# Attention and expert layer on one core: last transposes on TensorE, and the order of the first pairs and of the last pair's side work

## The chip, the cores and the metric

The kernel runs on one core of a Trainium2 chip. The core's engines run side by side, each through its own list of instructions in order: TensorE (PE, matmuls into the PSUM banks), VectorE (DVE), ScalarE (ACT), GpSimd (POOL), and SyncE (SP), which here only starts transfers. Transfers can be started from SP's, ScalarE's or GpSimd's queue and share 16 DMA engines. Engines wait for one another on semaphores. The metric is the device time of one execution, in microseconds (us), the median over several runs.

## What is computed

Attention over 8 batches, 8 heads and 1152 keys, with queries averaged in pairs (576 queries a head), and then a layer of 8 experts of which each of the 4608 tokens takes one.

```python
q_pool = q.reshape(B, H, S // 2, 2, D).mean(axis=3)          # B=8, H=8, S=1152, D=64
scores = np.matmul(q_pool, k.transpose(0, 1, 3, 2)) / np.sqrt(D)
attn = softmax(scores)                                       # over the 1152 keys
x = concat_heads(np.matmul(attn, v))                         # 4608 tokens x 512
logits = x @ w_gate + modality_bias[modality_id]
e_idx, gate = argmax(logits), softmax(logits)[argmax]
out[mask_e] = gate * (relu(x[mask_e] @ w1[e]) @ w2[e])       # for each expert e, F=1024
```

All data are float32. The kernel keeps the precision with 16-bit operands: each operand is split into a high half and a remainder (hi and lo, vh and vl, xh and xl), and a product is two or three matmuls.

## The kernel before

**Attention.** The work goes in 32 pairs: two batches of one head, their 64 rows side by side on the 128 partitions. A pair takes 18 steps (NSTEP), nine for each of its two heads, so the loop has 576 steps, and a written order (ORD, three strings used in turn) says what a step emits: "s" one bank of scores (`scores`: L821 and L822 into psc, exponential on ScalarE at L823), "v" one fifth of a value product (`pv`: L868 to L870), "M" and "X" pieces of the next pair's pass for the row maxima (`maxpass`: L759 and L760), "J" one step of a job, "F" what falls due. TensorE, ScalarE, VectorE and GpSimd keep exactly this order; SP's order is left to a scheduler. What belongs to other pairs is put at fixed steps by constants: T_KQ and T_K2 (loads of K and Q), T_SPLIT, T_QH, T_HI, T_LO (splits), T_MAX and T_M1 (row maxima), T_PLACE, T_P1 and T_P2 (`place`, copies by SP into the score operands B1 and B2), V0 and T_SQ to T_VS (the scale of the values and their split in VH, vl and VS).

**The exponentials** come out as 32-bit integers whose low half is turned into a third operand Pl by ScalarE ('A', L804) or VectorE ('D', L806), as LOWS lists it, and LOWS_LAST for the last pair.

**The first pair** is made in line ahead of the loop: K in thirds and Q in halves are loaded by turns; `first_max` takes the maxima of five of nine query tiles with 15 matmuls (L779) and reductions (L780); `row` reduces them (L731), transposes the result on TensorE (L735), scales it (L744) and has SP copy it as a row into B2. The first scores need this row. T_PRE pieces of the maxima of the other four tiles are emitted before the loop.

**After each two pairs** `split_xl` splits their outputs in xh and xl, and two DMA transposes (L851) make xt, from which `logits` takes the gate's logits (18 matmuls, L238). For the last pair the two transposes are issued from ScalarE's queue. When all four parts of a group of 1152 tokens are there, `route` computes expert and gate; after three groups `first_list` makes the list of tokens of the first six blocks of experts (`operands` on VectorE at L463 to L471, matmuls at L490, indices at L502 to L509). These run as generators, one piece at a time: a `yield n` puts the next piece n steps later. At step T_G0 of the last pair `gather_first` drains what is left of them and gathers the first block's tokens. T_X0 starts the turning of this block (`turn`), T_W0 its weights' loads, T_W1 their splits, W1D the steps by which the remainder follows.

**Experts.** 18 blocks of 256 tokens and one of 128: `gemm1` (L1191 to L1193), relu on ScalarE and its remainder on VectorE (hh L1196, hl L1197), `gemm2` (L1237 to L1239). The weights come in pieces of 512 KB through a ring of five buffers, each split by ScalarE and VectorE (L1174, L1175). Tokens are gathered by GpSimd, split (xs, L1141) and turned by DMA transposes on SP (L1147). Each half piece of a product calls `beside`, which takes one step of what is left from the attention: after SW empty steps the last `logits`, the last group's `route` and `other_list`.

Of the kernel before, what the change touches and what calls it, by code (L numbers as in the profile page):

```python
# [22 lines left out]
P = 128  # L23
# [19 lines left out]
T_LIST = -126  # L43
RS = 4
# [8 lines left out]
LOWS_LAST = (((0, 576, 'D', 1), (576, 1152, 'D', 2), (1152, 1728, 'A', 3)),)  # L53
D0 = 5
T_RT = 25
D2 = 3
T_K2 = 3
T_F = 7
T_P2 = 10
T_P1 = 5  # L60
T_M1 = 3
# [8 lines left out]
V0 = (0, 1, (2, 3), 4, (4, 5))  # L70
# [14 lines left out]
T_G0 = 0  # L85
T_X0 = 9
# [24 lines left out]
SW = 8  # L111
PR = 2
NF = 4
T_W0 = (1, 1, 2, 3)
W1D = 1
T_W1 = (7,9,11,13)
# [19 lines left out]
LLA = 4  # L136
# [3 lines left out]
T_PRE = 9  # L140
# [11 lines left out]
class Router:  # L152
# [11 lines left out]
    def setup(self, ids, w_gate, bias):  # L164
# [16 lines left out]
        nc.gpsimd.affine_select(out=self.up, in_=self.up, pattern=[[1, P]], compare_op=ALU.is_gt, fill=0.0, base=0, channel_multiplier=-1)  # L181
        self.on = con.tile([P, P], BF16, name="on")
# [46 lines left out]
    def logits(self, g, cc, x, w):  # L229

        nc = self.nc
        if g not in self.lg:
            self.lg[g] = self.keep.tile([P, NT, 3 * E], F32, name="lg")
# [297 lines left out]
def attention(tc, ctx, att, ident, npairs, xpool, on_two, on_split, on_scale, jobs, side, set_pm, started, ahead, hip):  # L531
# [54 lines left out]
    def split_q(p):  # L586
# [6 lines left out]
        if p == 0:  # L593
            q = t.rearrange("p (w n) -> p w n", w=2)
            for i in range(2):
                nc.vector.tensor_tensor(q[:, 0, half_q(i)], q[:, 0, half_q(i)], q[:, 1, half_q(i)], op=ALU.add)
        else:
            nc.gpsimd.tensor_tensor(t[:, 0:SQ], t[:, 0:SQ], t[:, SQ:S], op=ALU.add)
# [106 lines left out]
    def values(p, i, lo):  # L705
# [8 lines left out]
        if lo:  # L714
# [6 lines left out]
    def shifted(p):  # L721

        need(p, "vh0", "vh1")
        made.add((p, "vs"))
        nc.vector.tensor_single_scalar(flat(VS[p % 3])[:, :, 0:D], flat(VH[p % 3])[:, :, 0:D], 2.0 ** -16, op=ALU.mult)

    def row(p, mp, u0, u1):
# [13 lines left out]
        def put(pt):  # L741
# [3 lines left out]
            move(B2[p % 2][D:D + 1, 2 * S + u0 * P:2 * S + u1 * P], mr[0:n])  # L745
# [27 lines left out]
    def first_max(p):  # L773

        s = st[p]
        mp = sm.tile([P, 9, 3], F32, name="mp")
        for i, (u, t) in enumerate([(u, t) for us in ((0, 1), (2, 3, 4)) for t in range(3) for u in us]):
            pt = ps_sc.tile([P, 512], F32, name="psc") if i % 2 else ps_max.tile([P, 512], F32, name="pm")
            nc.tensor.matmul(pt[:, 0:384], QB[p % 2][:, u], s["hi"][:, t * 384:(t + 1) * 384], start=True, stop=True)  # L779
            nc.vector.tensor_reduce(mp[:, u, t:t + 1], pt[:, 0:384], op=ALU.max, axis=AX.X)  # L780
        row(p, mp, 0, 5)()
        return mp

    def scores(p, j, r):
# [10 lines left out]
        lows = (LOWS_LAST if p == npairs - 1 else LOWS)  # L795
# [47 lines left out]
    def split_xl(p, x2):  # L843
# [4 lines left out]
        if p % 2:  # L848
            xt = [xpool.tile([P, NT, P], F16, name=f"xt{i}", bufs=1) for i in range(2)]
            for i, x in enumerate((xh, xl)):  # L850
                (nc.scalar if p == npairs - 1 else nc.sync).dma_start_transpose(out=xt[i], in_=x.rearrange("p t d -> p (t d)"))  # L851
            on_split(p // 2, xt, st[p - 1]["both"].bitcast(F32))
# [133 lines left out]
    for p in range(npairs):  # L986
        b = NSTEP * p
        go = lambda t, f, *a, p=p, b=b, **k: at(b + t, p, lambda: f(p, *a), **k)
        if p > 1:
            d = D2 if p == 2 else 0  # L990
            go(T_K2 - b if p == 2 else T_KQ, load_kq, end=False)
            go(T_SPLIT + d, split_q)
            go(T_QH + d, split_qh)
            for i in range(2):
                go(T_HI[i] + d, split_hi, i)
            for i in range(3 if LOC else 7):
                go(T_LO[LOCI[i] if LOC else i] + d, split_lo, i)
            go(T_MAX + d, lambda p: mxq.append(maxpass(p)), end=False)
# [6 lines left out]
        sq, power_, vh, vs, vl = (T_SQ, T_POW, T_VH, T_VS, T_VL) if p else V0  # L1005
# [337 lines left out]
def attention_moe(tc, att, ids, w_gate, bias, w1, w2, out):  # L1343
    nc = tc.nc
    with ExitStack() as ctx:
# [106 lines left out]
```

## Time and profile before

| | |
|---|---|
| median of 3 runs (lowest, highest) | 1191.72 us (1188.98 to 1196.6) |
| the profiled execution | 1192.5 us |
| its span, first to last instruction | 1190.7 us |
| mean granted TensorE clock | 0.984 |
| first scores, first exponential | 19.42, 20.38 us |
| first matmul of the experts | 771.99 us |
| HBM read, written | 146.11 MB, 19.18 MB |

In the profile a row of the timeline is: start, duration, engine, line, operation, output<-input, shape, count, and in brackets the idle time before it with what ended that. "PEld" is the loading of weights into TensorE, "ACTq" and "SPq" are issues on a queue. In the view of stretches the columns are the stretch, its length, busy time with number of instructions of PE, PEld, DVE, ACT and POOL, the granted TensorE clock, the share of the DMA engines' time and GB/s.

### The profile page before, as it was taken

The numbers are of one execution on the slowest core, as the hardware profiler recorded it, in microseconds if no ns is written. First come the engines' busy times: TensorE is split into PE (matmuls) and PEld (weight loads), VectorE is DVE, ScalarE is ACT, GpSimd is POOL, SyncE is SP. The second block draws the span as 40 slices with busy tenths as digits, with TensorE's granted clock in tenths as the row PEclk, the third lists the DMA queues.
The fourth block names the chain that finished last, engine by engine and source line by source line (L and its number), as shares of the span: only waits on it lengthen the run. The fifth ranks groups of instructions, "written<-read, shape, count | busy, mean of one in ns | idle before, by whom it ended". The sixth has DMA issues, their size and how long they took to land. (4 is left out here: it accounts for less than half of the span.)

```text
span 1190.7 us, 36600 instructions
## 1 busy us (share of the span) xinstructions
PE 1117.9 (94%) x14944; PEld 817.8 (69%) x14944; DVE 984.2 (83%) x2033; ACT 918.1 (77%) x1461; POOL 408.3 (34%) x384
## 2 busy tenths in 40 slices
PE   5898999999999999999999989888999999999994
PEld 2566777777777777777777767755767666676763
DVE  6988899899999899999999999649996756667571
ACT  5778999999999999999998888736556656566561
POOL 6253444444434444434445331123213121211200
PEclk7999999999999999999999999899999999999998
DMA  7657768758759669668668534499999999999970
GB/s 221 183 134 169 156 170 203 149 159 199 165 156 217 150 164 205 148 163 187 169 167 186 145 93 110 142 186 279 230 300 309 298 278 278 286 280 274 261 243 22
DMA packets 177937, 233.25 MB, mean 196 GB/s; under 512 B 94719, under 2 KB 129167, under 8 KB 177760
## 3 DMA queue, kind: packets, MB, share of 16 engines
q1 hardware_dynamic: 169264, 210.46, 68.7%
q0 software_dynamic: 6128, 19.78, 6.5%
q10 hardware_dynamic: 2368, 0.59, 0.8%
q8 instruction: 119, 1.95, 0.7%
q14 instruction: 58, 0.48, 0.1%
HBM read 146.11 MB, written 19.18 MB: 139 GB/s over the span
## 5 line engine op out<-in xcount | busy, mean ns | idle before, releaser
L823 ACT ACTIVATE Pe<-psc 128x432 int32<-128x432 f32 x768 | 380.8, 526 | 71.4 <-PE psc L822 59.4
L760 DVE TENSOR_REDUCE mp<-pm 128x1 f32<-128x512 f32 x566 | 370.6, 684 | 9.7 <-PE pm L759 4.1
L868 PE MATMUL xp<-VH,Pe 128*128 128x65 f16 x2880 | 374.2, 194 | 0.5 <-ACT xfirst L1099 0.5
L870 PE MATMUL xp<-VS,Pl 128*128 128x65 f16 x2880 | 373.7, 193 | 0.0
L869 PE MATMUL xp<-vl,Pe 128*128 128x64 f16 x2880 | 372.4, 192 | 0.5 <-issue 0.5
L869 PEld LDWEIGHTS <-Pe 128*128 128x128 f16 x2880 | 268.3, 98 | 89.4 <-issue 1.6
L868 PEld LDWEIGHTS <-Pe 128*128 128x128 f16 x2880 | 272.8, 98 | 56.2 <-issue 18.6
L822 PE MATMUL psc<-B 65*128 65x432 f16 (+2 forms) x1152 | 307.4, 289 | 1.4 <-DMA B<-mr 1.1
L821 PE MATMUL psc<-B 128*128 128x432 f16 (+2 forms) x1152 | 306.9, 288 | 1.5 <-ACT Pe L823 1.5
L870 PEld LDWEIGHTS <-Pl 128*128 128x128 f16 x2880 | 267.2, 97 | 0.0
L759 PE MATMUL pm<-hi,QB 128*128 128x512 f16 x566 | 215.4, 382 | 19.3 <-DVE mp L760 16.3
L804 ACT ACTIVATE Pl<-Pe 128x1152 f16<-128x1152 uint16 (+1 forms) x192 | 220.6, 1149 | 6.1
L717 POOL TENSOR_SCALAR VH<-rawv,sc 128x512 f16<-128x512 f32 (+1 forms) x60 | 103.4, 1734 | 180.3 <-PE xp L870 110.6
L633 POOL TENSOR_TENSOR lo<-rawk,hi 128x576 f16<-128x576 f32 (+1 forms) x68 | 89.0, 1312 | 221.0 <-ACT hi L617 170.7
L1191 PE MATMUL ph<-xpart,w1h 128*128 128x256 f16 x544 | 148.9, 274 | 6.7 <-DVE hl L1197 5.6
L1192 PE MATMUL ph<-xpart,w1h 128*128 128x256 f16 x544 | 148.9, 274 | 0.0
L1193 PE MATMUL ph<-xpart,w1l 128*128 128x256 f16 x544 | 148.9, 274 | 0.0
L822 PEld LDWEIGHTS <-B 65*128 65x128 f16 x1152 | 113.7, 99 | 25.6 <-issue 2.4
L821 PEld LDWEIGHTS <-B 128*128 128x128 f16 x1152 | 113.2, 98 | 11.6 <-issue 6.2
L806 DVE TENSOR_SCALAR Pl<-Pe 128x576 f16<-128x576 uint16 x198 | 104.4, 528 | 15.5 <-ACT Pe L823 14.3
L1237 PE MATMUL po<-w2h,hh 128*128 128x512 f16 x296 | 112.9, 381 | 0.0
L1238 PE MATMUL po<-w2l,hh 128*128 128x512 f16 x296 | 112.7, 381 | 0.0
(254 smaller groups left out, 1782.3 us busy)
## 6 DMA issues: line engine op xcount, KB each, us to landing
w2r<-in_w_dram SPq DMA_DIRECT2D x76, 512.0 KB
w1r<-in_w_dram SPq DMA_DIRECT2D x72, 512.0 KB
rawv<-in_att_dram SPq DMA_DIRECT2D x32, 576.0 KB
B<-hi SPq DMA_DIRECT2D x128, 144.0 KB
rawq<-in_att_dram SPq DMA_DIRECT2D x31, 576.0 KB
rawk<-in_att_dram SPq DMA_DIRECT2D x31, 576.0 KB
B<-qh SPq DMA_DIRECT2D x128, 72.0 KB
B<-lo SPq DMA_DIRECT2D x64, 144.0 KB
```

What stands on the lines that cost most here:

```text
L759: nc.tensor.matmul(pm, QB[p % 2][:, u], s["hi"][:, t * 512:(t + 1) * 512], start=True, stop=True)
L760: nc.vector.tensor_reduce(mp[:, u, t:t + 1], pm, op=ALU.max, axis=AX.X)
L804: nc.scalar.activation(low, rest, AF.Copy, scale=LOW)
L821: nc.tensor.matmul(o, b1[:, ks], b1[:, qs], start=True, stop=False, skip_group_check=True)
L822: nc.tensor.matmul(o, b2[:, ks], b2[:, qs], start=False, stop=True, skip_group_check=True)
L823: nc.scalar.activation(Pe[:, D + x0:D + x1], pt, AF.Exp, scale=1.0 / 16)
L868: nc.tensor.matmul(out, Ph[:, qs], vh[:, c, j, 0:D + 1], start=c == 0 and g == 0, stop=False, skip_group_check=True)
L869: nc.tensor.matmul(out[:, 0:D], Ph[:, qs], vl[:, c, j], start=False, stop=False, skip_group_check=True)
L870: nc.tensor.matmul(out, Pl[:, qs], vs[:, c, j, 0:D + 1], start=False, stop=c == NKC - 1, skip_group_check=True)
L1191: nc.tensor.matmul(o, hi[:, c, fs], xh[:, :, c], start=c == 0, stop=False)
L1192: nc.tensor.matmul(o, hi[:, c, fs], xl[:, :, c], start=False, stop=False)
L1193: nc.tensor.matmul(o, lo[:, c, fs], xh[:, :, c], start=False, stop=c == 3)
```

## The change

The last pair's xh and xl are transposed by matmuls with an identity (`turned`) in place of the two DMA transposes, as part of the last job, which starts after 3 empty steps in place of 8. The first pair's loads, query sums and maxima are emitted in a new order; its row goes by ScalarE's queue; seven pieces of its other maxima move into the loop. The second pair's square, scale and split move from the first steps to steps 7 to 15. For the first two pairs the values' remainder is two operations on GpSimd in place of one on VectorE, and the first pair's VS is made on ScalarE. `route` and the lists wait fewer steps between pieces. In the last pair ScalarE's part of Pl goes to VectorE, and the first block's gather, turning and splits get other steps. LOWS0, for the first pair, equals what was used before.

```diff
-T_LIST = -126
-RS = 4
+T_LIST = -127
+RS = 2
...
-LOWS_LAST = (((0, 576, 'D', 1), (576, 1152, 'D', 2), (1152, 1728, 'A', 3)),)
+LOWS_LAST = (((0, 864, 'D', 1), (864, 1728, 'D', 3)),)
...
-D2 = 3
-T_K2 = 3
+D2 = (4, 2, 2, 3, 6)
+T_K2 = 0
...
-T_P2 = 10
-T_P1 = 5
-T_M1 = 3
+T_P2 = 4
+T_P1 = 7
+T_M1 = 5
...
-V0 = (0, 1, (2, 3), 4, (4, 5))
+V0 = (0, 1, (2, 3), 3, (3, 4))
+V1 = (7, 9, (12, 13), 14, (14, 15))
+LOWS0 = (((0, 1152, 'A', 2), (1152, 1728, 'D', 3)),)
...
-T_G0 = 0
-T_X0 = 9
+T_G0 = -1
+T_X0 = 7
...
-SW = 8
+SW = 3
...
-T_W0 = (1, 1, 2, 3)
-W1D = 1
-T_W1 = (7,9,11,13)
+T_W0 = (1, 3, 2, 3)
+W1D = 0
+T_W1 = (6, 4, 10, 11)
...
-LLA = 4
+LLA = 1
...
-T_PRE = 9
+T_PRE = 2
...
+        self.id16 = con.tile([P, P], F16, name="id16")
+        nc.gpsimd.tensor_copy(self.id16, self.ident)
...
-    def logits(self, g, cc, x, w):
+    def turned(self, x, o):
 
         nc = self.nc
+        for i in range(2):
+            for a, b in ((0, 4), (4, 8), (8, NT)):
+                pt = self.pm(0)[:, 0:(b - a) * P].rearrange("p (t n) -> p t n", n=P)
+                for t in range(a, b):
+                    nc.tensor.matmul(pt[:, t - a], x[i][:, t], self.id16, start=True, stop=True, skip_group_check=True)
+                (nc.vector.tensor_copy if i else nc.scalar.copy)(o[i][:, a:b], pt)
+                yield
+
+    def logits(self, g, cc, x, w, to=None):
+
+        nc = self.nc
+        if to:
+            yield from self.turned(x, to)
+            x = to
...
-            for i in range(3):
-                if i < 2:
+            for x, i in ((q, 0), (k, 0), (k, 1), (q, 1), (k, 2)):
+                if x is q:
                     nc.sync.dma_start(out=two(q)[:, :, half_q(i)], in_=two(att[p, :, S:2 * S])[:, :, half_q(i)])
-                nc.sync.dma_start(out=k[:, i * 384:(i + 1) * 384], in_=att[p, :, i * 384:(i + 1) * 384])
+                else:
+                    nc.sync.dma_start(out=k[:, i * 384:(i + 1) * 384], in_=att[p, :, i * 384:(i + 1) * 384])
...
-        if lo:
+        if lo and p < 2:
+            nc.gpsimd.tensor_scalar(v, v, s["sc"], None, op0=ALU.mult)
+            nc.gpsimd.tensor_tensor(flat(s["vl"][:, c]), v, vh, op=ALU.subtract)
+        elif lo:
             nc.vector.scalar_tensor_tensor(flat(s["vl"][:, c]), v, s["sc"], vh, op0=ALU.mult, op1=ALU.subtract)
...
-        nc.vector.tensor_single_scalar(flat(VS[p % 3])[:, :, 0:D], flat(VH[p % 3])[:, :, 0:D], 2.0 ** -16, op=ALU.mult)
+        o, v = (flat(x[p % 3])[:, :, 0:D] for x in (VS, VH))
+        if p:
+            nc.vector.tensor_single_scalar(o, v, 2.0 ** -16, op=ALU.mult)
+        else:
+            nc.scalar.activation(o, v, AF.Copy, scale=2.0 ** -16)
...
-            move(B2[p % 2][D:D + 1, 2 * S + u0 * P:2 * S + u1 * P], mr[0:n])
+            (nc.sync if p or u0 else nc.scalar).dma_start(out=B2[p % 2][D:D + 1, 2 * S + u0 * P:2 * S + u1 * P], in_=mr[0:n])
...
             nc.vector.tensor_reduce(mp[:, u, t:t + 1], pt[:, 0:384], op=ALU.max, axis=AX.X)
+            yield
         row(p, mp, 0, 5)()
-        return mp
...
+            both = st[p - 1]["both"].bitcast(F32)
+            if p == npairs - 1:
+                on_split(p // 2, (xh, xl), both, xt)
+                return
             for i, x in enumerate((xh, xl)):
-                (nc.scalar if p == npairs - 1 else nc.sync).dma_start_transpose(out=xt[i], in_=x.rearrange("p t d -> p (t d)"))
-            on_split(p // 2, xt, st[p - 1]["both"].bitcast(F32))
+                nc.sync.dma_start_transpose(out=xt[i], in_=x.rearrange("p t d -> p (t d)"))
+            on_split(p // 2, xt, both)
...
-    for i in range(3):
+    first = first_max(0)
+    for n, i in ((0, 0), (2, 1), (2, 2)):
         if i < 2:
-            nc.scalar.copy(qb[0:D, half_q(i)], q0[0:D, half_q(i)])
+            both = st[0]["q"].rearrange("p (w n) -> p w n", w=2)
+            nc.vector.tensor_tensor(both[:, 0, half_q(i)], both[:, 0, half_q(i)], both[:, 1, half_q(i)], op=ALU.add)
+        if i == 0:
+            nc.scalar.copy(qb[0:D, half_q(0)], q0[0:D, half_q(0)])
         split_hi(0, i)
+        if i == 1:
+            nc.scalar.copy(qb[0:D, half_q(1)], q0[0:D, half_q(1)])
+        for _ in range(2):
+            next(first)
...
-    mp0 = first_max(0)
     place_lo(0, (1,), 1)
     place_k(0, (1,))
     if npairs > 1:
...
             split_lo(1, i)
+    drain(first)
+    mp0 = st[0]["mp"]
...
-        sq, power_, vh, vs, vl = (T_SQ, T_POW, T_VH, T_VS, T_VL) if p else V0
+        sq, power_, vh, vs, vl = (T_SQ, T_POW, T_VH, T_VS, T_VL) if p > 1 else V1 if p else V0
+        if p == 1:
+            go = lambda t, f, *a, p=p: at(t, p, lambda: f(p, *a))
```

D2's five values are added to the steps of the third pair's query sum, query split, key splits, remainders and maxima, where one value was added before.

More of the change, by code (lines that the diff above doesn't have):

```diff
@@ L592, in split_q @@
         s["lo"] = pa.tile([P, KQ], F16, name="lo")
[L593 to L597, printed above, removed]
+        if p:
             nc.gpsimd.tensor_tensor(t[:, 0:SQ], t[:, 0:SQ], t[:, SQ:S], op=ALU.add)
@@ L724, in shifted @@
         made.add((p, "vs"))
-        nc.vector.tensor_single_scalar(flat(VS[p % 3])[:, :, 0:D], flat(VH[p % 3])[:, :, 0:D], 2.0 ** -16, op=ALU.mult)
+        o, v = (flat(x[p % 3])[:, :, 0:D] for x in (VS, VH))
+        if p:
+            nc.vector.tensor_single_scalar(o, v, 2.0 ** -16, op=ALU.mult)
+        else:
+            nc.scalar.activation(o, v, AF.Copy, scale=2.0 ** -16)
     def row(p, mp, u0, u1):
@@ L775, in first_max @@
         s = st[p]
-        mp = sm.tile([P, 9, 3], F32, name="mp")
+        mp = s["mp"] = sm.tile([P, 9, 3], F32, name="mp")
         for i, (u, t) in enumerate([(u, t) for us in ((0, 1), (2, 3, 4)) for t in range(3) for u in us]):
@@ L794, in scores @@
         s["P", j, r] = (word(F16, 1), Pl, i % NR)
-        lows = (LOWS_LAST if p == npairs - 1 else LOWS)
+        lows = LOWS_LAST if p == npairs - 1 else LOWS if p else LOWS0
         lows = lows[i % len(lows)]
@@ L989, in attention @@
         if p > 1:
-            d = D2 if p == 2 else 0
+            d = D2 if p == 2 else (0,) * 5
             go(T_K2 - b if p == 2 else T_KQ, load_kq, end=False)
-            go(T_SPLIT + d, split_q)
-            go(T_QH + d, split_qh)
+            go(T_SPLIT + d[0], split_q)
+            go(T_QH + d[1], split_qh)
             for i in range(2):
-                go(T_HI[i] + d, split_hi, i)
+                go(T_HI[i] + d[2], split_hi, i)
             for i in range(3 if LOC else 7):
-                go(T_LO[LOCI[i] if LOC else i] + d, split_lo, i)
-            go(T_MAX + d, lambda p: mxq.append(maxpass(p)), end=False)
+                go(T_LO[LOCI[i] if LOC else i] + d[3], split_lo, i)
+            go(T_MAX + d[4], lambda p: mxq.append(maxpass(p)), end=False)
             go(T_PLACE + (T_P2 if p == 2 else 0), place, end=False)
@@ L1364, in on_two, with on_split @@
                     side.append(rt.other_list())
-        def on_split(n, xt, isc):
+        def on_split(n, xt, isc, to=None):
             g, cc = divmod(n, H // 2)
-            jobs.append(rt.logits(g, cc, xt, rt.gate_weights(cc, isc)))
+            jobs.append(rt.logits(g, cc, xt, rt.gate_weights(cc, isc), to))
         def set_pm(f):
```

## The prediction

> **What bounds the kernel now.** I read the page's busy shares first, then the busy time by stretch, then TensorE's waits, and only then the order in time around each wait.
>
> ```profile
> PE 1117.9 (94%) x14944; PEld 817.8 (69%) x14944; DVE 984.2 (83%) x2033; ACT 918.1 (77%) x1461; POOL 408.3 (34%) x384
> ...
> 200.00:600.00 400.00, 393.36 (x6804) 304.01 (x6800) 376.50 (x847) 375.37 (x636) 172.89 (x139) 1.00 0.74 173
> ...
> 740.00:750.00 10.00, 7.45 (x130) 6.36 (x128) 6.79 (x28) 4.62 (x10) 1.66 (x2) 0.79 0.68 220
> 750.00:760.00 10.00, 10.00 (x187) 8.24 (x185) 5.40 (x14) 8.57 (x16) 0.71 (x1) 0.87 0.21 55
> ...
> 900.00:1000.00 100.00, 100.00 (x684) 66.67 (x682) 67.48 (x81) 61.22 (x79) 24.67 (x21) 1.00 1.03 291
> ...
> PE px L1210 <- DVE hl L1213: 1.0, 1, 1.0
> ```
>
> Columns of a stretch: its length, then busy time and instructions of TensorE, its weight loads, VectorE, ScalarE and GpSimd, the granted TensorE clock, the DMA share, GB/s. TensorE is the bound in the long stages: 393 of 400 us in the attention, 100 of 100 in the experts, where the only wait after 850 us is the last row's 1.0. So time saved counts only where TensorE stands still or runs at a lower clock: the head (to about 40 us), 740 to 760, and 784 to 820. A microsecond won there should shift all that follows. The change works at exactly these three places.
>
> **The seam between attention and experts (784 to 829).** This is the largest term.
>
> ```profile
> 771.99 0.28 PE L1191 MATMUL ph<-xfirst,w1h 128*128 128x256 f16 x1
> ...
> 782.47 0.38 PE L1237 MATMUL po<-w2h,hh 128*128 128x512 f16 x1
> ...
> 784.84 0.38 PE L1239 MATMUL po<-w2h,hl 128*128 128x512 f16 x1
> 789.32 0.19 PE L238 MATMUL pmr<-wgs,xt 128*128 128x24 bf16 x1 [4.10 <-ACT w2h L1174]
> 790.10 0.63 PE L238 MATMUL pmr<-wgs,xt 128*128 128x24 bf16 x17 [0.59 <-DMA xt<-x]
> ...
> 800.99 0.27 PE L1191 MATMUL ph<-xpart,w1h 128*128 128x256 f16 x1 [1.05 <-DMA xpart<-xs]
> ...
> 814.62 0.37 PE L1191 MATMUL ph<-xpart,w1h 128*128 128x256 f16 x1 [5.56 <-DVE hl L1197]
> ...
> 829.21 0.27 PE L1191 MATMUL ph<-xpart,w1h 128*128 128x256 f16 x1
> ...
> 774.24 1.47 ACTq L851 DMA_TRANSPOSE xt<-x  x1
> 775.78 8.62 ACTq L851 DMA_TRANSPOSE xt<-x  x1
> 784.45 0.31 ACT L219 ACTIVATE wgs<-wg,both 128x24 bf16<-128x24 bf16 x1 [8.09 <-issue]
> ...
> 796.90 1.06 ACT L1174 ACTIVATE w1h<-w1r 128x1024 f16<-128x1024 f32 x1 [4.74 <-DMA w1r<-in_w_dram]
> ...
> SPq L1147 <- DMA xt<-x: 15.0, 1, 15.0
> ```
>
> Issuing the last two DMA transposes holds ScalarE from 774.24 to 784.40. Three things follow. The logits matmul (L238), which stands in TensorE's order amid block 0, waits from about 785.05 to 790.10. The next block's transposes on SP's queue wait 15.0 us, with the weight loads behind them. And ScalarE, held up and then waiting 4.74 us for weights, makes hh and hl so late that TensorE waits 5.56 us in block 1.
>
> A block without waits takes 10.48 us for its first product (771.99 to 782.47) and 4 x 2.59 us for its second (12 matmuls from 782.47 to 784.84 + 0.22), so 20.8. Block 0 and its wait last 29.0 (771.99 to 800.99), block 1 28.2 (to 829.21): together 15.6 over. The change puts in place of the DMA transposes 18 matmuls of 128 columns and six evictions, three on ScalarE and three on VectorE.
>
> ```profile
> 33.49 0.38 PE L767 MATMUL pm<-hi,QB 128*128 128x128 f16 x4
> ...
> 33.71 0.23 PE L821 MATMUL psc<-B 128*128 128x144 f16 x1
> ...
> 785.62 0.57 ACT L1196 ACTIVATE hh<-ph 128x512 f16<-128x512 f32 x1
> ```
>
> Four such matmuls take 0.22 us (33.49 to 33.71), so 18 take 1.0. An eviction of 512 columns takes 0.57 at most, and ScalarE, free from about 774, has the room. SW at 3 starts them at the fourth call of the side work instead of the ninth, so they and the logits fall inside block 0. What stays of the 15.6: these 1.0, the logits' own 0.6, and 2.5 for what is late next: block 1's xs (L1141) waits on ScalarE for its gather, and the second eviction stands behind it while only two PSUM buffers serve the transposes (2), and the routing matmuls of block 1 (0.5). That leaves 11.5. Upper end 13.5 (no new wait); lower end 7 (block 1 keeps its wait, since its weights still come one behind the other through SP).
>
> The Trainium skill, Advanced Engine Details and Errata, "X-Bar Transpose (TRN2)", says that transposing DMAs are as fast as regular ones, at 350 to 400 GB/s. By that, the two of 288 KB would cost an estimated 1.7 us and their removal would save next to nothing; the sum would then be about 1184. The rows above differ, with 10.1 us of issue and a landing near 790, so I give it no chance of its own.
>
> **The list before the first gather (743 to 752).**
>
> ```profile
> 743.06 0.60 PE L490 MATMUL pm<-r,ol 128*128 128x24 bf16 x18
> ...
> 747.04 0.43 PE L821 MATMUL psc<-B 128*128 128x288 f16 x1
> ...
> 743.55 0.18 DVE L493 COPY accA<-pm 128x24 f32<-128x24 f32 x1
> ...
> 747.85 0.17 DVE L509 SCALAR_TENSOR_TENSOR siA<-mA,vA 128x12 int32<-128x12 f32 x1
> ```
>
> At step T_G0 of the last pair (558) everything left of the side work is drained at once. The first thing drained is the copy of group 0 (L493), so the list stands just behind its first matmuls, and by its yields 1 + 3 + 18 + 1 + 3 + 4 + 1 + 3 = 34 steps of it are left: three pairs of operands on VectorE, with matmuls that wait for them. TensorE resumes the scores at 747.04, 3.4 us after its matmuls of 743.06 to 743.66, and the clock falls to 0.79 and 0.87 in the two stretches above: 10 x 0.21 + 10 x 0.13 = 3.4 us of work lost. RS 4 to 2 takes 16 steps out of the route, LLA 4 to 1 takes 3 from it and 3 from the list; T_G0 one step earlier gives one back. So 13 of the 34 steps are left: one set of o and r, 18 matmuls, adds and indices. I keep 1 us of wait and no loss of clock, 5.8 gained; of VectorE's 4.5 us (743.55 to 748.02) some 2.5, the operands, move into the pair before, where VectorE is busy too: 1.8 paid back. Term 4; ends 2 (operands pay in full, some clock lost) and 6. T_LIST is passed long before and costs nothing.
>
> **The last pair.** LOWS_LAST moves six pieces from ScalarE to VectorE, and W1D, T_W1, T_X0 bring splits and first block earlier.
>
> ```profile
> 760.00:770.00 10.00, 8.16 (x157) 6.83 (x155) 8.06 (x16) 9.91 (x20) 1.72 (x2) 1.00 0.30 88
> ...
> 750.42 0.68 ACT L804 ACTIVATE Pl<-Pe 128x576 f16<-128x576 uint16 x1
> ```
>
> ScalarE is full there (9.91) and TensorE loses 1.8. The pieces free 6 x 0.68 = 4.1 us of ScalarE, but VectorE takes them and, with W1D at 0, waits for each w1h in line. I take 0.5, ends -2 and +2.
>
> **The head.**
>
> ```profile
> 15.09 0.28 DVE L744 TENSOR_SCALAR mr<-pj 5x128 f16<-5x128 f32 x1 [0.45 <-PE pj L735]
> 15.40 0.84 SPq L565 DMA_DIRECT2D B<-mr  x1
> 19.42 0.56 PE L821 MATMUL psc<-B 128*128 128x432 f16 x1
> 20.38 0.53 ACT L823 ACTIVATE Pe<-psc 128x432 int32<-128x432 f32 x1 [5.69 <-PE psc L822]
> 22.83 0.16 PE L685 MATMUL pm<-ss,ones 128*128 128x1 bf16 x1 [1.04 <-ACT vl L679]
> 24.85 0.16 PE L685 MATMUL pm<-ss,ones 128*128 128x1 bf16 x1 [1.86 <-ACT vl L679]
> ...
> 40.00:70.00 30.00, 27.28 (x475) 21.11 (x473) 26.46 (x55) 22.99 (x39) 15.92 (x31) 1.00 0.52 122
> ...
> 42.72 0.46 DVE L806 TENSOR_SCALAR Pl<-Pe 128x576 f16<-128x576 uint16 x1
> ...
> 44.41 1.28 POOL L633 TENSOR_TENSOR lo<-rawk,hi 128x576 f16<-128x576 f32 x1 [15.73 <-ACT hi L617]
> 44.80 1.22 DVE L806 TENSOR_SCALAR Pl<-Pe 128x576 f16<-128x576 uint16 x1
> ...
> L717 POOL TENSOR_SCALAR VH<-rawv,sc x58: 1562/1877/2152, 56.1 to 699.9; 128x512 f16<-128x512 f32 x29, 128x640 f16<-128x640 f32 x29
> L715 DVE SCALAR_TENSOR_TENSOR vl<-rawv,sc,VH x4: 745/856/884, 31.4 to 50.1; 128x640 f16<-128x640 f32 x2, 128x512 f16<-128x512 f32 x2
> ```
>
> T_PRE 9 to 2 lets the first scores start once the first row lands; they stood behind nine pieces until 19.42. The row is 15.40 at issue and there by 19.78 at the latest, so the gain lies between 0 and 3 us: on ScalarE's queue it passes the five copies (one lo, two K, two Q) that SP now issues ahead of that point. Behind it on ScalarE stands only the first exponential, which needs it anyway. Loading the halves of Q around K gives VectorE two reductions earlier, but it then waits for the last third of K: about 0.4 us. The second pair's square and sum leave steps 0 and 1, where TensorE waited 1.86 for them: 2 us. Together about 4. The first pair's VS (L725) moves to ScalarE, which idles there.
>
> The remainders cost VectorE 4 x 0.86 = 3.4 us and GpSimd, in two operations each, about 8 x 1.6 = 12.8 (median 1.88 of a scaling, 1.28 of a subtraction). The first pair's run while GpSimd idles; the second pair's, 6.4 us from step 14, are due from step 21 on, in the stretch 40 to 70, where GpSimd is busy 15.92 of 30. But its operations hold VectorE: the L806 of 44.80 takes 1.22 us beside a GpSimd operation of 44.41 to 45.69, where 0.46 is usual. Eight new ones at 0.76 are up to 6 us held. Against that stand the delayed second maxpass (T_M1, T_P1 and D2 by two or three steps; no time where VectorE stays full) and SP's order of loads (T_K2, T_P2), which cost nothing while copies land a pair ahead; if they don't, row 15.40's 4.4 us is the price. I take 3 for the head; ends -1 and 7.
>
> The Trainium skill, SBUF — State Buffer, "Who interferes with whom", makes this an exclusive lock that VectorE and GpSimd take for a whole instruction. By that rule every VectorE operation of the kinds it names is held, the head wins nothing, and the sum would be 1176, as in rival 2; the trace agrees as far as the row of 44.80 goes.
>
> **Sum.** 11.5 + 4 + 0.5 + 3 = 19. The profiled run took 1192.5 us (span 1190.7, 1.8 around it), 0.8 above the median of 1191.72: 1192.5 - 19 = 1173.5, less 0.8 gives 1173.
>
> **Rivals.**
> 1. Weights bound the experts. For it: the DMA share of 1.03 at 291 GB/s. Against it: no TensorE wait after 850 in the rows. Then block 1 keeps its lag, and of the seam only block 0's 5.0 us less the new matmuls and one wait, 3, is won; with the other 7.5 that makes 1181; chance 0.17, within 1%.
> 2. GpSimd holds VectorE for all eight operations: head 0, 1176; chance 0.25.
> 3. Slower: GpSimd is too slow for the second pair's remainders. TensorE's products take vl in order, so each microsecond late is one lost, and the queue behind it makes the third pair's operands. Of the 30 us from 40 to 70 GpSimd has 14 free, so 6.4 us fit. Lateness decides against the change only past 19 us, when the four operations take 14 + 19 = 33 us, five times their rows: 1192 and over; at six times, 1197. No row of GpSimd's exceeds 2.2 us. Chance 0.04.
>
> My forecast, with the head's gain kept, has 0.54. Forecast and rival 2 give 0.79 for faster by over 1% (below 1179.8; 1% is about what a measurement of this kernel tells from no change); I put 0.02 of this to same for the low ends together: 0.77, 0.19, 0.04. All upper ends, 28.5, give 1163; all lower ends, 6, give 1186, and rival 1 lies inside.
>
> **What would show it.** Seam: no DMA transposes on ScalarE's queue after 770, block 0 to block 1 in 22 to 24 us, the 15.0 wait gone, and the 5.56 wait below 2. List: at most 1.5 us between L490 and the scores, clock 1.00 from 740 to 760. Head: first exponential near 18 to 19, and second L685 no longer before step 2. I am wrong if ScalarE's wait for w1r grows at block 1 (rival 1), if L806 rows over 1 us fill the first 50 us (rival 2), or if L869 waits for vl (rival 3).

## The result, and the profile after

The changed kernel takes 1171.34 us (median of 4 runs, 1171.18 to 1173.55), the kernel before 1191.99 (4 runs, 1188.98 to 1196.6): a ratio of 0.983, with a 95% interval from 0.981 to 0.986. The prediction was 1173 us, in a range from 1163 to 1186. The profiled run after took 1171.42 us, its span 1169.7.

The page of the changed kernel, busy shares, and below them its stretches (length; then busy time and instructions of TensorE, its weight loads, VectorE, ScalarE, GpSimd; granted TensorE clock; DMA share; GB/s):

```profile
PE 1113.4 (95%) x14962; PEld 816.2 (70%) x14962; DVE 985.5 (84%) x2031; ACT 918.1 (78%) x1459; POOL 417.3 (36%) x393
```

```profile
200.00:600.00 400.00, 392.64 (x6784) 303.53 (x6782) 375.47 (x849) 374.51 (x634) 171.91 (x137) 1.00 0.74 173
600.00:700.00 100.00, 92.49 (x1572) 70.72 (x1569) 97.87 (x245) 87.62 (x147) 43.12 (x37) 1.00 0.62 151
740.00:750.00 10.00, 9.82 (x204) 8.15 (x201) 7.04 (x22) 8.41 (x15) 2.57 (x2) 1.00 0.77 264
750.00:760.00 10.00, 9.14 (x179) 7.80 (x176) 9.55 (x19) 9.13 (x20) 2.57 (x2) 1.00 0.33 94
900.00:1000.00 100.00, 100.00 (x684) 66.68 (x682) 66.72 (x78) 60.83 (x78) 20.17 (x19) 1.00 1.04 291
```

The same view of the kernel before, for the one stretch that the prediction did not show:

```profile
600.00:700.00 100.00, 94.76 (x1612) 72.56 (x1609) 97.31 (x242) 89.73 (x151) 42.41 (x37) 1.00 0.65 160
```

The reader is to see three things. The attention from 200 to 600 and the experts are what they were: TensorE still binds there. From 740 to 750 TensorE now works 9.82 of 10 us, at a clock of 1.00, where it had 7.45 at 0.79. And from 600 to 700 it works *less* than before (92.49 against 94.76), with VectorE at 97.87 (97.31 before): something was paid there.

To say how much, time marks are better than busy shares. VectorE takes a reciprocal of the sums twice a pair, once for each head (L913 after the change, L887 before), and all 64 are in every trace. The start of a pair's second one is taken here as the end of the pair; pairs count from 0. Three of these marks and the first matmuls of the first three expert blocks, after the change:

```profile
108.22 0.19 DVE L913 RECIPROCAL rr<-rs 128x5 f32<-128x5 f32 x1
...
580.20 0.19 DVE L913 RECIPROCAL rr<-rs 128x5 f32<-128x5 f32 x1
...
701.39 0.19 DVE L913 RECIPROCAL rr<-rs 128x5 f32<-128x5 f32 x1
...
763.22 0.28 PE L1228 MATMUL ph<-xfirst,w1h 128*128 128x256 f16 x1
...
787.99 0.27 PE L1228 MATMUL ph<-xpart,w1h 128*128 128x256 f16 x1
...
809.10 0.27 PE L1228 MATMUL ph<-xpart,w1h 128*128 128x256 f16 x1
```

and the first three marks of the kernel before:

```profile
112.40 0.19 DVE L887 RECIPROCAL rr<-rs 128x5 f32<-128x5 f32 x1
...
583.80 0.19 DVE L887 RECIPROCAL rr<-rs 128x5 f32<-128x5 f32 x1
...
701.69 0.19 DVE L887 RECIPROCAL rr<-rs 128x5 f32<-128x5 f32 x1
```

Differences between these marks divide the 21.0 us of span (1190.7 less 1169.7):

| Stretch | Before, us | After, us | Won |
|---|---|---|---|
| start to the end of pair 2 | 112.4 | 108.2 | 4.2 |
| end of pair 2 to end of pair 23 | 471.4 | 472.0 | -0.6 |
| end of pair 23 to end of pair 28 | 117.9 | 121.2 | -3.3 |
| end of pair 28 to the first expert block | 70.3 | 61.8 | 8.5 |
| blocks 0 and 1 | 57.2 | 45.9 | 11.3 |
| the rest | 361.5 | 360.6 | 0.9 |

The seam, which is the row of blocks 0 and 1, is the term forecast (11.5). The third and the fourth row belong together: the list before the first gather no longer stops TensorE in the last pairs, but the work of the route and the list on VectorE has moved ahead, into pairs 25 to 28, and is paid there. TensorE's waits from 12 to 52 us show the first row; in us in total, times, longest, first before and then after:

```profile
PE pm L759 <- DVE mp L760: 3.4, 6, 1.4
PE pm L685 <- ACT vl L679: 2.9, 2, 1.9
```

```profile
PE pm L781 <- DVE mp L782: 1.0, 4, 0.4
PE psc L844 <- DMA B<-mr: 0.9, 1, 0.9
```

The wait for the second pair's square (L685) is gone, the waits of the maximum's matmuls (L759, now L781) are 2.4 us less, and a wait of 0.9 for the first row, B from mr, is new.

### The profile page after: what moved, and what is told of

It is laid out like the page before. It is cut to its first block, busy times and chain, and to the rows that moved or that the text cites. A ratio compares the mean times of both kernels' runs of the same rounds, so it can differ in the third digit from the quotient of the medians.

```text
span 1169.7 us, 36628 instructions
## 1 busy us (share of the span) xinstructions
PE 1113.4 (95%) x14962; PEld 816.2 (70%) x14962; DVE 985.5 (84%) x2031; ACT 918.1 (78%) x1459; POOL 417.3 (36%) x393
## 5 line engine op out<-in xcount | busy, mean ns | idle before, releaser
L782 DVE TENSOR_REDUCE mp<-pm 128x1 f32<-128x512 f32 x566 | 369.8, 683 | 13.7 <-PE pm L781 8.2
L781 PE MATMUL pm<-hi,QB 128*128 128x512 f16 x566 | 215.4, 383 | 17.6 <-DVE mp L782 13.6
L826 ACT ACTIVATE Pl<-Pe 128x1152 f16<-128x1152 uint16 x186 | 216.5, 1164 | 5.9
L828 DVE TENSOR_SCALAR Pl<-Pe 128x576 f16<-128x576 uint16 (+1 forms) x198 | 108.1, 546 | 8.5 <-ACT Pe L845 7.1
L1276 PE MATMUL po<-w2h,hl 128*128 128x512 f16 x296 | 112.2, 379 | 0.0
```

What stands on the lines that cost most here:

```text
L781: nc.tensor.matmul(pm, QB[p % 2][:, u], s["hi"][:, t * 512:(t + 1) * 512], start=True, stop=True)
L782: nc.vector.tensor_reduce(mp[:, u, t:t + 1], pm, op=ALU.max, axis=AX.X)
L826: nc.scalar.activation(low, rest, AF.Copy, scale=LOW)
```

## The experiments

All twelve kernels were timed beside the kernel before; the ratios below are to it, with their 95% intervals, so 0.983 is the changed kernel. One limit must be known first. From the end of pair 2 to that of pair 23 the fourteen profiled executions took 470.2 to 478.8 us, with nearly the same code there. Part of it is one stretch, which five of them (e1, e3, e7, e9 and e11) pass some 2.5 us more slowly; here in the changed kernel and in e3:

```profile
140.00:150.00 10.00, 9.47 (x151) 7.02 (x150) 7.83 (x21) 9.48 (x17) 3.59 (x3) 1.00 1.07 195
```

```profile
140.00:150.00 10.00, 8.09 (x108) 5.63 (x105) 6.15 (x14) 7.31 (x13) 2.65 (x2) 0.83 0.97 184
```

What makes this stretch differ was not found. So a difference of 3 us in a total says little by itself, and the parts are read from the marks, each from one execution:

| Kernel | Pair 2 ends | 23 to 28 | 28 to block 0 | Blocks 0 and 1 |
|---|---|---|---|---|
| before | 112.4 | 117.9 | 70.3 | 57.2 |
| after | 108.2 | 121.2 | 61.8 | 45.9 |
| e1 DMA transposes again | 110.1 | 121.6 | 61.6 | 55.8 |
| e2 seam alone | 111.5 | 117.2 | 69.2 | 45.8 |
| e3 old list | 108.7 | 118.0 | 67.1 | 45.8 |
| e4 remainders on VectorE | 107.4 | 121.5 | 62.0 | 45.8 |
| e5 old start | 112.8 | 121.5 | 63.8 | 46.0 |
| e6 first row on SP | 108.7 | 121.1 | 62.4 | 46.3 |
| e7 second pair's square early | 113.3 | 121.3 | 63.9 | 45.8 |
| e8 old last pair | 107.8 | 121.3 | 62.2 | 46.5 |
| e9 ten pieces to ScalarE | 108.6 | 121.4 | 61.6 | 46.0 |
| e10 list on GpSimd | 105.3 | 130.6 | 72.3 | 45.8 |
| e11 evictions on ScalarE | 108.1 | 121.2 | 62.6 | 44.6 |
| e12 as e7, loads in the old order | 108.2 | 120.7 | 62.9 | 45.8 |

How much a mark can tell is seen where kernels have the same code. The seven with the new start untouched (after, e1, e3, e8 to e11) end pair 2 between 105.3 and 110.1. All with the new list on VectorE take 120.7 to 121.6 from pair 23 to 28, and those that also have the new last pair 61.6 to 63.9 from there to block 0 and, but for e1 and e11, 45.8 to 46.3 for blocks 0 and 1. Smaller differences are not told from zero below.

**e1: the last transposes by DMA again.**

```diff
-SW = 3
+SW = 8
-            if p == npairs - 1:
-                on_split(p // 2, (xh, xl), both, xt)
-                return
             for i, x in enumerate((xh, xl)):
-                nc.sync.dma_start_transpose(out=xt[i], ...)
+                (nc.scalar if p == npairs - 1 else nc.sync).dma_start_transpose(out=xt[i], ...)
```

> The changed kernel, but with the last two transposes by DMA from ScalarE's queue again, and SW at 8 (the logits at the ninth call of the side work). Theory (the DMA transposes' issue is what stretched the first two blocks): the seam's 11.3 us come back, 1171.3 + 11.3 = 1182.6 us; first experts matmul stays near 763, block 0 about 29 us instead of 24.8, block 1 about 28 instead of 21.1, with waits of 4 to 5 us for the logits and in block 1. Rival (the first blocks were late because their weights came late, and these now come some 9 us earlier with the end of the attention): at most 4 us come back, under 1176, with block 1 near 22 us.

Measured: 1181.78 us (0.991, 0.990 to 0.993). The profiled execution was a longer one than the median (span 1188.9, with 478.8 from pair 2 to pair 23), but its blocks tell the story: 55.8 us for the two, 9.9 more than after the change. ScalarE's queue and TensorE's and SP's waits:

```profile
774.32 1.80 ACTq L874 DMA_TRANSPOSE xt<-x  x1
776.19 6.78 ACTq L874 DMA_TRANSPOSE xt<-x  x1
```

```profile
PE ph L1225 <- DVE hl L1231: 5.8, 2, 5.3
PE pmr L256 <- DMA xt<-x: 3.2, 2, 2.6
```

```profile
SPq L1181 <- DMA xt<-x: 14.3, 1, 14.3
```

All three signs of the kernel before are back: the long issue on ScalarE, SP's wait, and both waits of TensorE. The rival's condition, weights coming earlier, was given here as well, and it did not help. The rival falls. By the Trainium skill, Advanced Engine Details and Errata, "X-Bar Transpose (TRN2)", transposing DMAs are as fast as regular ones. The prediction's estimate from that left next to nothing to win, and e1 disagrees with it by some 10 us.

**e2: the seam alone, on the kernel before.**

```diff
+        self.id16 = con.tile([P, P], F16, name="id16")
+        nc.gpsimd.tensor_copy(self.id16, self.ident)
+    def turned(self, x, o):
...
-SW = 8
+SW = 3
```

> The kernel before with the transposes on TensorE and SW at 3, and nothing else of the change. Theory: the seam is independent of the rest, so 1192 - 11.3 = 1180.7 us, with the attention's milestones those of the kernel before (first experts matmul near 772). Rival (the seam's gain needs the weights of the first blocks to be loaded and split earlier, as the change's T_W0, T_W1 and T_X0 do): under 8 us, above 1184, with ScalarE's wait for w1r in block 1 longer than 4 us.

Measured: 1180.78 us (0.991, 0.989 to 0.993). Blocks 0 and 1 take 45.8 us, as with the whole change, although start, list and last pair are those of the kernel before. Taken away and added alone, the part has nearly the same size (9.9 and 11.4 us): the seam is independent of the rest. SW and the transposes were changed together in both runs, so what SW alone is worth is not shown.

**e3: the list as it was.**

```diff
-T_LIST = -127
-RS = 2
+T_LIST = -126
+RS = 4
-T_G0 = -1
+T_G0 = 0
-LLA = 1
+LLA = 4
```

> The changed kernel with RS, LLA, T_G0 and T_LIST as they were. By the prediction's term: 4 us slower, 1175.3. Theory from the trace of the changed kernel (the list's operands, 4.5 us of VectorE, now pay in full in pairs 21 to 28, where VectorE is full): the burst and the low clock come back before pair 30 (5.5 to 6.6 us), but pairs 21 to 28 lose about 5 us less, so 1 to 2 us slower, about 1173. Rival (the loss of pairs 21 to 28 has another cause, the new order of the first pairs or a drift): it stays, and the kernel is about 6 us slower, 1177.

Measured: 1173.38 us (0.984, 0.982 to 0.986). The marks agree with the total: 5.3 us more from pair 28 to the first block, 3.2 us less from pair 23 to 28, so 2.1 in sum. The burst is back in the stretch, and VectorE's operands r are what the list's matmuls wait for (a group's view: who made the engine sit idle, us and times):

```profile
740.00:750.00 10.00, 7.44 (x129) 6.32 (x128) 6.10 (x25) 4.34 (x10) 2.81 (x2) 0.83 0.68 236
```

```profile
L508 PE MATMUL pm<-r,ol x27: 172/173/180, 720.1 to 741.1; 128*128 128x24 bf16 x27
...
  DVE mp L782: 0.6, 1
```

```profile
L508 PE MATMUL pm<-r,ol x27: 172/173/183, 740.7 to 744.3; 128*128 128x24 bf16 x27
...
  DVE r L489: 2.6, 3
```

The upper group is the changed kernel's, the lower e3's. Spread from 720 to 741 us the list's 27 matmuls wait 0.6 us; drained at once from 740.7 they wait 2.6. The loss between pairs 23 and 28 goes with these four constants: e3 is without it, like e2 and the kernel before, and all others with the new list have it. The rival falls.

The same marks, pair by pair, with the summed time of VectorE's operations of the route and the list (L272 to L527) in each:

| Pair | Length after, us | Length in e3 | Route and list after, us | in e3 |
|---|---|---|---|---|
| 25 | 24.6 | 23.0 | 3.8 | 1.0 |
| 26 | 24.1 | 23.2 | 3.3 | 3.2 |
| 27 | 27.1 | 24.7 | 6.2 | 4.3 |
| 28 | 23.2 | 24.5 | 3.5 | 5.0 |
| 29 | 25.2 | 26.3 | 3.4 | 4.8 |
| 30 | 19.9 | 24.5 | 4.8 | 7.9 |

From pair 25 to 28 VectorE has 3.3 us more of this work than in e3, and the four pairs take some 3.5 us more. So what is moved here is paid in full. The theory named the operands, but the first of them starts at 672.5, in pair 27: pairs 25 and 26 lose 2.5 us to the route's pieces alone.

**e4: the first two pairs' remainders on VectorE.**

```diff
-        if lo and p < 2:
-            nc.gpsimd.tensor_scalar(v, v, s["sc"], None, op0=ALU.mult)
-            nc.gpsimd.tensor_tensor(flat(s["vl"][:, c]), v, vh, op=ALU.subtract)
-        elif lo:
+        if lo:
```

> The changed kernel with the remainders of the first two pairs on VectorE again (four operations of about 0.86 us in place of eight on GpSimd). Theory (moving them off VectorE helps, for the first 60 us are bound by it): 3.4 us of VectorE come back less the 2 to 3 us that GpSimd's operations hold it, so 0 to 1.5 us slower, about 1172; the start of pair 2's products (108.2) shifts by as much. Rival 2 of the prediction (GpSimd's operations hold VectorE as long as they run): 2 to 4 us faster, about 1168.5, and no row of the pieces of the low half above 1 us before 50 us.

Measured: 1172.32 us (0.984, 0.982 to 0.986); pair 2 ends 0.8 us earlier, if anything. Why the move is worth nothing is seen in the changed kernel, VectorE first and GpSimd below:

```profile
35.61 1.52 DVE L828 TENSOR_SCALAR Pl<-Pe 128x576 f16<-128x576 uint16 x1
...
44.10 1.42 DVE L828 TENSOR_SCALAR Pl<-Pe 128x576 f16<-128x576 uint16 x1
...
47.39 1.07 DVE L828 TENSOR_SCALAR Pl<-Pe 128x576 f16<-128x576 uint16 x1 [0.99 <-ACT Pe L845]
```

```profile
43.63 1.57 POOL L731 TENSOR_TENSOR vl<-rawv,VH 128x640 f16<-128x640 f32 x1
...
47.03 1.11 POOL L731 TENSOR_TENSOR vl<-rawv,VH 128x512 f16<-128x512 f32 x1
```

GpSimd's two subtractions end at 45.20 and 48.14 (start plus time), and the pieces of 44.10 and 47.39 end at 45.52 and 48.46, 0.32 us later each. They take 1.42 and 1.07 us where 0.46 is usual: 1.6 us held of the 3.4 that VectorE is spared. The longest row, 35.61, ran beside another GpSimd operation, and e4 has one row of 1.53 us too. Neither the theory's loss nor the rival's gain is told from zero.

**e5: the whole old start.** The kernel before with the changed seam, list and last pair.

```diff
-D2 = (4, 2, 2, 3, 6)
-T_K2 = 0
+D2 = 3
+T_K2 = 3
-T_P2 = 4
-T_P1 = 7
-T_M1 = 5
+T_P2 = 10
+T_P1 = 5
+T_M1 = 3
-T_PRE = 2
+T_PRE = 9
...
```

> The changed kernel with the whole start of the kernel before (its order of loads and halves, the first row on SP's queue behind nine pieces, the second pair's values at the old steps, all remainders and the first pair's VS on VectorE, T_K2, T_P2, T_P1, T_M1 and D2 as they were); seam, list and last pair as changed. By the prediction's term: 3 us slower, 1174.3. Theory from the traces (pair 2 begins 4.2 us and pair 10 about 5 us earlier with the new start): 4 to 5 us slower, 1175.8, with pairs 2 to 22 late by that throughout. Rival (rival 2 of the prediction: the new start is worth nothing, and the shift in the traces is the low clock that the profiled run before had in its first 30 us): 0 to 1 us, under 1172.5.

Measured: 1177.23 us (0.987, 0.984 to 0.989). Pair 2 ends 4.6 us later than after the change, at 112.8, near the 112.4 and 111.5 of the two other kernels with the old start. The rival falls: in their first 30 us these three were granted 1.00 (e5), 0.77 (before) and 0.89 (e2), and pair 2 ended within 1.3 us of the same time. Part of the rest of the 5.9 us between the totals lies from pair 28 to block 0, 2.0 longer. ScalarE waits there for the first weights, 2.28 us where it is 0.55 after the change, and one bank of scores then waits 1.91 for ScalarE:

```profile
754.20 1.06 ACT L1413 ACTIVATE w1h<-rawk 128x1024 f16<-128x1024 f32 x1 [2.28 <-DMA rawk<-in_w_dram]
```

e7, where pair 2 ends as late, has the same wait (2.43). Why these weights come later was not looked into.

**e6: the first row on SP's queue.**

```diff
-            (nc.sync if p or u0 else nc.scalar).dma_start(out=B2[p % 2]..., in_=mr[0:n])
+            nc.sync.dma_start(out=B2[p % 2]..., in_=mr[0:n])
```

> The changed kernel with the first row on SP's queue again, behind what SP has been given by then. Theory: the row lands up to 3 us later, the first scores and the first exponential with it (19 to 21 instead of 18.0), and the kernel is 1 to 2 us slower, about 1173. Rival (the first scores are held by VectorE's and TensorE's own work, and the row was in time on either queue): first exponential within 0.5 us of 18.0, and the same time.

Measured: 1171.74 us (0.982, 0.980 to 0.984). The first scores wait for the row as the theory has it,

```profile
PE psc L844 <- DMA B<-mr: 3.4, 1, 3.4
```

the first exponential starts at 19.88 instead of 18.01, and pair 0 ends 1.9 us later (62.1 against 60.2; the seven with the new start lie between 57.5 and 61.4). But pair 2 ends only 0.5 later and the total is 0.4 longer, neither told from zero. So the wait is real, and of the 1 to 2 us that the theory put on it nothing is seen in the time.

**e7 and e12: the second pair's square and sum early, with the loads in the new and in the old order.**

```diff
-V1 = (7, 9, (12, 13), 14, (14, 15))
+V1 = (0, 1, (12, 13), 14, (14, 15))
```

and in e12 also

```diff
-T_K2 = 0
+T_K2 = 3
```

> The changed kernel with the second pair's square and sum at steps 0 and 1 again instead of 7 and 9. Theory (they stood in TensorE's order and made it wait 1.86 us): the wait is back before 27 us, and pair 1 begins about 2 us later, 1173.3. Rival (TensorE waits there for VectorE anyway, so the wait only takes the place of another): pair 1 within 0.7 us of 49.2, and the same time.

> As e7 (the second pair's square and sum at steps 0 and 1), and with the third pair's loads at step 3 again (T_K2 at 3 instead of 0), so that SP asks for the second pair's V ahead of the third pair's Q and K, as in the kernel before. Theory (e7's wait of 5.9 us in place of 1.9 came from the V that stands behind two 590 KB loads; the two moves belong together): ScalarE's wait for rawv falls from 5.5 us to about 1, TensorE's wait for the second square to about 2 us, and pair 1 begins 2 to 3 us earlier than in e7 (54.4), near 52. Rival (the V is late whatever stands ahead of it, because other transfers fill the memory's bandwidth at this time): the wait stays above 4 us and pair 1 begins at 54 or later.

Measured: e7 1178.47 us (0.987, 0.985 to 0.989), e12 1172.17 us (0.984, 0.981 to 0.987). ScalarE and SP's queue in e7:

```profile
26.89 1.16 ACT L694 ACTIVATE vl<-rawv 128x1152 f16<-128x1152 f32 x1 [5.49 <-DMA rawv<-in_att_dram]
```

```profile
18.70 0.53 SPq L598 DMA_DIRECT2D rawq<-in_att_dram  x1
19.27 0.44 SPq L599 DMA_DIRECT2D rawk<-in_att_dram  x1
19.76 0.43 SPq L603 DMA_DIRECT2D rawv<-in_att_dram  x1
```

and in e12:

```profile
22.24 1.16 ACT L694 ACTIVATE vl<-rawv 128x1152 f16<-128x1152 f32 x1 [1.04 <-DMA rawv<-in_att_dram]
```

```profile
17.80 0.58 SPq L603 DMA_DIRECT2D rawv<-in_att_dram  x1
18.49 0.40 SPq L598 DMA_DIRECT2D rawq<-in_att_dram  x1
```

With the third pair's Q and K asked for ahead of it, the second pair's V is 4.6 us later, TensorE waits 5.9 us and pair 2 ends at 113.3. In the old order the wait is 1.5 us and pair 2 ends at 108.2, as after the change. So with both moves taken back nothing is lost, and e7's 5 us are the price of the earlier loads without the later square: the later square is what the earlier loads need. The later square without the earlier loads was not run.

**e8: the last pair as it was.**

```diff
-LOWS_LAST = (((0, 864, 'D', 1), (864, 1728, 'D', 3)),)
+LOWS_LAST = (((0, 576, 'D', 1), (576, 1152, 'D', 2), (1152, 1728, 'A', 3)),)
-T_W0 = (1, 3, 2, 3)
-W1D = 0
-T_W1 = (6, 4, 10, 11)
-T_X0 = 7
+T_W0 = (1, 1, 2, 3)
+W1D = 1
+T_W1 = (7,9,11,13)
+T_X0 = 9
```

> The changed kernel with LOWS_LAST, T_W0, T_W1, W1D and T_X0 as they were; list and seam as changed. By the prediction's term: 0.5 us slower, 1171.8. Theory from the traces (from pair 30 to the first experts matmul 50.8 us before and 42.1 after, of which the list explains some 6): 2 to 3 us slower, about 1174, with ScalarE full again from 750 to the end of the attention. Rival (the earlier splits are worth nothing, since the weights were there in time): the same time, within 0.7 us.

Measured: 1173.83 us (0.984, 0.981 to 0.986); from pair 28 to the first block 62.2 us against 61.8. By the marks the rival is nearer: 0.4 us there and 0.6 in blocks 0 and 1, hardly more than such marks differ. The total is 2.5 us longer, as the theory had it, but its six runs spread from 1170.61 to 1177.08. So with the new list the last pair's new order is worth between nothing and 2.5 us. With the old list it is perhaps 2.7 (69.8 for the mean of the kernel before and e2, 67.1 in e3), from one execution of each.

**e9: ten pieces of pairs 24 to 28 moved to ScalarE.**

```diff
+LOWS_MID = (((0, 1152, 'A', 2), (1152, 1728, 'A', 3)),)
-        lows = LOWS_LAST if p == npairs - 1 else LOWS if p else LOWS0
+        lows = LOWS_LAST if p == npairs - 1 else LOWS_MID if 24 <= p < 29 and r == 0 else LOWS if p else LOWS0
```

> The changed kernel, with the smaller piece of the low halves (576 columns, 0.46 us on VectorE) of one group in three of the pairs 24 to 28 given to ScalarE: ten pieces. Theory (in pairs 24 to 28 TensorE waits because VectorE is full with the list and the route, 98 of 100 us, while ScalarE has 12 of 100 free): VectorE gets 4.6 us back, the way from pair 24 to pair 29 shrinks from 121.2 to about 118, and the kernel is 3 us faster, 1168.3. Rival (these pairs are slow for the order of the steps, or because pieces on ScalarE come later than on VectorE): 120 us or more there, and the same time.

Measured: 1174.64 us (0.985, 0.983 to 0.987); 121.4 us from pair 23 to 28. The stretch 640 to 680 after the change and in e9:

```profile
640.00:680.00 40.00, 36.60 (x615) 27.71 (x613) 39.08 (x103) 33.79 (x56) 15.42 (x11) 1.00 0.49 131
```

```profile
640.00:680.00 40.00, 35.56 (x596) 26.89 (x593) 38.65 (x100) 36.59 (x61) 12.53 (x11) 1.00 0.64 155
```

The theory falls. VectorE gets 0.4 us of 40 back, ScalarE takes 2.8, and TensorE does 1 us less. A busy share of 98% on VectorE did not mean that ScalarE's idle 12% were to be had. Which order of the steps holds there was not tried.

**e10: the list's operands on GpSimd.**

```diff
-POOL_LISTS = ()
+POOL_LISTS = (12,)
```

> The changed kernel with the operands of the list before the first gather built on GpSimd (81 small operations) instead of VectorE. Theory (VectorE's time is the price that the list pays in pairs 25 to 29): VectorE gets some 4 us back and the kernel is 1 to 3 us faster, about 1169.5. Rival (GpSimd's operations hold VectorE as long as they run, and are slower): 1 to 4 us slower, with VectorE's operations longer than usual beside them.

Measured: 1190.13 us (0.999, 0.998 to 1.001), 19 us lost. Groups of GpSimd between 660 and 735 us (shapes and count, then busy us and mean ns), and TensorE's waits from 660 to 770:

```profile
L472 POOL TENSOR_SCALAR ol<-lane,lof 128x128 bf16<-128x128 f32 x27 | 17.8, 660 | 5.1 <-DVE lof L458 5.1
L474 POOL TENSOR_SCALAR r<-col,hif,part 128x12 bf16<-128x12 f32 x27 | 12.8, 474 | 2.0
L474 POOL TENSOR_SCALAR r<-col,hif 128x12 bf16<-128x12 f32 x27 | 10.6, 394 | 2.2
```

```profile
PE pm L781 <- DMA QB<-qh: 12.3, 2, 7.5
```

41.2 us of new work stand in GpSimd's queue among its other work, and the splits of the queries (qh) and their copies into QB come late: two waits, 12.3 of the 19 us. The rival had the sign and not the mechanism: it is GpSimd's own queue that is late, not VectorE that is held. VectorE's pieces of 576 columns (L828) take 507 ns in the mean between 660 and 735, in e10 as after the change.

**e11: all six evictions on ScalarE.**

```diff
-                (nc.vector.tensor_copy if i else nc.scalar.copy)(o[i][:, a:b], pt)
+                nc.scalar.copy(o[i][:, a:b], pt)
```

> The changed kernel with all six evictions of the transposes on ScalarE instead of three on VectorE. Theory (TensorE's 1.5 us wait in block 0 is for the eviction behind VectorE's splits, and ScalarE idles 3.5 us right after): the wait goes, block 0 shrinks from 24.8 to about 23.3, and the kernel is 1 to 1.5 us faster, 1170. Rival (the next operation of VectorE or the weights are late instead, and block 1 grows by what block 0 wins): the first two blocks together stay at 45.9 us within 0.4.

Measured: 1172.55 us (0.984, 0.982 to 0.986). Block 0 takes 23.4 us instead of 24.8, and block 1 stays at 21.1. TensorE's waits from 764 us, after the change and in e11:

```profile
PE pmr L240 <- DVE xt L241: 1.5, 1, 1.5
...
PE pmr L240 <- ACT xt L241: 0.5, 1, 0.5
```

```profile
PE pmr L240 <- ACT xt L241: 0.5, 1, 0.5
```

The 1.5 us wait is gone and block 1 gives nothing back; the seam is 1.3 us shorter, as the theory has it. The total does not show it: its median is 1.2 us above that of the changed kernel. It is the one improvement on the change that the marks show, and no run shows that it makes the kernel faster.

## Why the prediction was right

**The seam (11.5; measured 11.3).** Shown by e1 and e2 from both sides. The signs named came: no DMA transposes on ScalarE's queue, block 0 in 24.8 us (a little over the 22 to 24 forecast), the 15.0 wait gone, no 5.56 wait. What stays of the 15.6 is 4.3, of which the prediction kept 4.1. The 2 us that it allowed for evictions are there, but not all where it put them: it had ScalarE's second eviction behind xs, and TensorE waits 0.5 for that one and 1.5 for VectorE's first, which stands behind its splits (e11). ScalarE still waits for weights late in block 0, but no wait of TensorE follows from it:

```profile
781.07 1.06 ACT L1211 ACTIVATE w1h<-w1r 128x1024 f16<-128x1024 f32 x1 [3.45 <-DMA w1r<-in_w_dram]
```

**Rival 1, weights bound the experts: falls.** At 291 GB/s and a DMA share of 1.04 TensorE works 100 of 100 us from 900 on; e1 gives the same weights and loses the seam.

**The list (4) and the last pair (0.5): right together, with sizes that cancel.** With the list changed first, as the prediction reckons, the stretch from pair 28 falls from 69.8 (mean of the kernel before and e2) to 62.2 (e8), 7.6 us, and that from pair 23 to 28 grows from 117.5 to 121.3, 3.8: the list wins 3.8 of the 4 forecast, and the last pair 0.4 more (e8 against the change), which is not told from zero. But the prediction had 5.8 gained less 1.8 paid back, and both are about 1.9 short. (Its 5.8 also counts the idle 2.55 us of 740 to 750 as time at the low clock, some 0.5 too much.) The step that failed is "1.8 paid back". It moves only 2.5 us of operands, into one pair, and asks no price for the route's pieces. The table by pairs shows 3.3 us more of VectorE's work from pair 25 to 28 than in e3, paid with 3.5, and the first 2.5 before any operand. That VectorE's time sets the length of these pairs is argued from this match; e9, which took 4.6 us of other work off VectorE, won nothing there, so the order of the steps has a part in it that is not shown. In the other order the last pair wins 2.7 and the list only 2.1 (e3). If both figures are good to the microsecond, the two remove part of the same stall, so their sum stands and the division doesn't. That the two errors of the list's term cancel is luck. The signs named came too: the scores follow the list's last matmuls at once,

```profile
740.83 0.44 PE L508 MATMUL pm<-r,ol 128*128 128x24 bf16 x7
...
741.30 0.35 PE L843 MATMUL psc<-B 128*128 128x432 f16 x1
```

and the clock from 740 to 760 is 1.00.

**The start (3; measured about 4).** e5 confirms the size by pair 2's end: the three kernels with the old start have it at 111.5 to 112.8, the seven with the new one at 105.3 to 110.1, 4.1 earlier in the mean. The terms behind it do not hold one by one: the row on ScalarE's queue shows 1.9 us at pair 0 and 0.5 at pair 2, where that is not told from zero (forecast 0 to 3 for the row's part), and the second pair's square, forecast at 2, is worth nothing that can be told together with the third pair's loads (e12). Most of the 4 must then lie in the rest: fewer pieces ahead of the first scores, the first maxima taken in step with the halves, the first pair's VS on ScalarE, and the second maximum later, whose matmuls wait 2.4 us less. These were not run apart, and which of them counts stays open. That this sum came out is partly chance.

**Rival 2, GpSimd holds VectorE: half right.** Three pieces of the low half took over 1 us, and the remainders' move is worth nothing (e4). But the rest of the start did not depend on it, so its price, the whole term, was not due. The Trainium skill, SBUF — State Buffer, "Who interferes with whom", describes such a lock; the rows of 44.10 and 47.39 agree with it, since both pieces end 0.32 us after the GpSimd operation beside them. VectorE's reductions were not held in the rows looked at: two in line (L782) take 1.28 us beside a GpSimd operation, from 48.38, and 1.28 while GpSimd idles, from 40.11. Other kinds of operations were not looked at, and it did not decide the total.

**Rival 3, GpSimd too slow: falls as priced.** The remainders' rows are 2.18 us at most and TensorE waits nowhere for vl. e10 shows what the same mechanism does with 41 us of new work in place of 13.

**The sum.** 19 forecast, 20.65 by the medians. Start, list, last pair and seam as measured in the traces give 4.2 - 3.3 + 8.5 + 11.3 = 20.7; the two rows left of the table, -0.6 and 0.9, belong to no part of the change.

## What to carry to other kernels

Look for the instruction that is expensive to *issue*: two DMA transposes stood ten microseconds in ScalarE's queue, and what they cost was seen as waits of TensorE and of SP's queue. Side work that is spread out instead of drained is not free: here it cost about as much time as it took on the nearly full engine that it moved to earlier pairs, and the gain is what the end wins less that. Price all of the work that moves, not only the pieces that were waited for. And when parts of a change are undone one at a time, check whether one made room for the other: e7 priced a move at 5 us that was worth nothing once the load that it answers to was moved back as well.

## What the runs showed of the hardware that was not expected

- The issue of a DMA transpose varied much: 1.47 and 8.62 us for the two on ScalarE's queue in the kernel before, 1.80 and 6.78 in e1.
- In e10 the list's operands cost GpSimd 660 ns for 128 columns, 27 times. After the change VectorE makes three at once, of 384 columns, in 649 ns:

```profile
L481 DVE TENSOR_TENSOR ol<-lof,lane 128x384 bf16<-128x384 f32 x9 | 5.8, 649 | 0.0
```

- The granted clock of the first 30 us differed between executions of nearly the same start (1.00 after the change, 0.77 in e6), and pair 2 ended within 0.5 us of the same time. In these two a lower clock there cost nothing that can be told.
